# Long-convolution block: taps in 64x64 tiles, half of v turned by DMA and half loaded as rows, all table sines first

## The chip, the cores and the metric

The kernel runs on one core of a Trainium2 chip. Its time is the device time of one execution in microseconds (us). PE is TensorE (matmuls), with PEld its weight loads; DVE is VectorE, ACT is ScalarE, POOL is GpSimd, and SP issues most of the DMAs. PSUM is where matmuls write; the working memory is SBUF, with 128 partitions.

## The reference: what is computed

`q`, `k`, `v` are 2048 tokens by 512 channels, in bf16. The block normalizes `q`, shifts `k` by a four-tap filter per channel, multiplies by `v`, convolves along the tokens with a filter as long as the sequence (by FFT), multiplies by the normalized `q`, adds the input, and then runs an MLP with 1376 hidden units on the normalized result.

```python
for t in range(ks):                                   # ks = 4
    k_shift = k_shift + k_pad[:, t:t + S, :] * shift_k[:, ks - 1 - t][None, None, :]
kv = k_shift * v
...
y_f = kv_f * kf_f[None, :, :, :]                      # rfft of kv and of ssm_k, length 2 * S
...
y = y + kv * ssm_D[None, None, :]
return q * y                                          # q is layernorm(A_q)
...
h = x + _A_ref(_layernorm(x, axis=-1), A_k, A_v, A_shift_k, A_ssm_k, A_ssm_D)
h2 = h + _B_ref(_layernorm(h, axis=-1), B_w1, B_w2)   # relu(x @ w1) @ w2
```

## The kernel before

The FFT is done as matmuls with tables of sines, in two stages forward and two back. The 512 channels are four groups of 128. Tokens are numbered as 32 rows by 64. "Rows" of the data have one partition for each of 32 blocks of 64 tokens, four channel groups below each other, which makes 128 partitions.

Every engine runs its instructions in the order in which the program records them, and waits on semaphores for what the others produce. So the order of the work is written out by hand, as a list of calls at L425 to L470. PSUM work goes through `bank2` (L278), which hands out four slots of two banks each, alternating between two pools; a slot is free again when its eviction is done. DMAs run in the order of the queue that issues them.

The stages, in order of time:

- **Loads** (L99 to L130): the filter rows `kfl` in eight DMAs (four from SP, four from ACT, the last two of ACT behind the first sines), then, on SP, `k` and `v` in four chunks of 512 tokens each, both turned by the DMA so that channels lie on partitions (`kT`, `vT`), then 512 tokens of the input (`x0`) and `w1`.
- **Tables** (L133 to L269): POOL writes index patterns, DVE turns them into angles modulo one turn (`turns2`, two operations of 1024), ACT takes the sine (`sines2`) into `tab`, POOL writes the negated halves (`negated`). Two of the four tables are made ahead of stage 1, two between its blocks.
- **Stage 1 of the filter** (`stage1`, L297): eight blocks, each of 64 matmuls with 32-row weights and 64 columns, plus four small ones for the direct term. Two PSUM slots a block, one evicted by ACT and one by DVE, into `a1k`.
- **Taps** (`taps`, L335): eight groups (four chunks by two halves of the channels). A tap is a matmul with a diagonal 128x128 matrix `wdiag` (made by POOL at L209): 8 matmuls of 512 columns a group. DVE multiplies the PSUM result by `vT`, in place (L342, 1024 elements).
- **Second stage of the filter** (`second_k`, L360): 16 groups of 8 matmuls, each evicted by ACT or DVE.
- **Rows** (`to_rows`, L285): PE turns `vT` (now `kv`) from channels to tokens on partitions, eight transposes of f32 words in each of four groups, and DVE writes each to `xfl` (L290, 1024 words).
- **Paired stage 1 of the data** (`stage1_pairs`, L320), eight blocks of 32 matmuls into `a1x`, evicted by ACT and DVE. It needs all of `xfl`.
- **Products** (`product`, L484): 16 groups: two second-stage groups in PSUM, multiplied by `a1k` by DVE (L493) and by DVE or, by way of a copy `usb` of ACT (L492), by POOL (L498).
- **Inverse** (L516 to L531), **last stage and gate** (L543 to L590), and the **MLP** (L627 to L694), whose matmuls fill PE to the end.

Channel order: within each group of 128 channels, the first 64 belong to half d=0 and the other 64 to half d=1, in all four groups.

Of the kernel before, what the change touches and what calls it, by code (L numbers as in the profile page):

```python
# [9 lines left out]
ALU = mybir.AluOpType  # L10
# [5 lines left out]
P = 128  # L16
# [39 lines left out]
def kernel(  # L56
# [36 lines left out]

    kfl = front.tile([P, 64, 2, 64], BF16, name="kfl")

    def load_rows(eng, rg):
        for d in range(2):
            src = bass.AP(tensor=A_ssm_k.tensor, offset=A_ssm_k.offset + S * (P * rg + 64 * d), ap=[[64, 32], [S, 64], [1, 64]])
            eng.dma_start(out=kfl[32 * rg:32 * rg + 32, :, d, :], in_=src)  # L99

    wsh = consts.tile([P, DC, KS], BF16, name="wsh")
    nc.scalar.dma_start(out=wsh[:], in_=A_shift_k.rearrange("(r p) j -> p r j", p=P))
    scratch = rows.tile([P, 4096], I32, tag="r", name="scratch")
    drow = scratch[:, 4064:4096].bitcast(BF16)
    nc.gpsimd.memset(drow, 0.0)
# [4 lines left out]
    vT = front.tile([P, DC, S], BF16, name="vT")  # L110
    CH = 512
    kT = [front.tile([P, DC, CH + 16], BF16, name=f"kT{c}") for c in range(4)]
    nc.vector.memset(kT[0][:, :, 0:16], 0.0)
    for c in range(4):
        if c == 0:
            nc.sync.dma_start_transpose(out=kT[c][:, :, 16:CH + 16], in_=k_d[0:CH, :])
        else:
            nc.sync.dma_start_transpose(out=kT[c][:], in_=k_d[CH * c - 16:CH * c + CH, :])
        nc.sync.dma_start_transpose(out=vT[:, :, CH * c:CH * c + CH], in_=v_d[CH * c:CH * c + CH, :])

    x0 = front.tile([P, 4, D], BF16, name="x0")
    for b, src in enumerate(_tokens(x_d, 0, 4)):
        nc.sync.dma_start(out=x0[32 * b:32 * b + 32].rearrange("p t d -> p (t d)"), in_=src)


    w1 = w1p.tile([P, DC, DFF], BF16, name="w1")
    for i in range(2):
        for d in range(2):
            nc.sync.dma_start(out=w1[64 * i:64 * i + 64, 2 * d:2 * d + 2],
                                in_=B_w1.rearrange("(c i d g) f -> i d g c f", c=2, i=2, d=2)[i, d])  # L130
# [29 lines left out]
    for s in range(0, P, 64):  # L160
        nc.gpsimd.iota(n2i[s:s + 64, :], pattern=[[0, 1]], base=0, channel_multiplier=1)
    r2 = scratch[:, 0:1024].rearrange("p (a b) -> p a b", b=64)
    nc.gpsimd.iota(r2, pattern=[[2, 16], [128, 64]], base=1, channel_multiplier=0)
    ident = consts.tile([P, P], BF16, name="ident")
# [3 lines left out]

    identw = consts.tile([P, P], F32, name="identw")
    nc.gpsimd.memset(identw[:], 0.0)  # L170
    nc.gpsimd.affine_select(out=identw[:], in_=identw[:], compare_op=ALU.not_equal, fill=1.0,
                            base=0, pattern=[[-1, P]], channel_multiplier=1)

    ind = consts.tile([P, P], BF16, name="ind")
    nc.gpsimd.memset(ind[:], 0.0)
    for s in range(0, P, 32):
        nc.gpsimd.affine_select(out=ind[s:s + 32, :], in_=ind[s:s + 32, :], compare_op=ALU.not_equal, fill=1.0,
                                base=0, pattern=[[-1, P]], channel_multiplier=4)

# [11 lines left out]
    load_rows(nc.scalar, 3)  # L191
    f1hi = consts.tile([P, 64], BF16, name="f1hi")
# [10 lines left out]
    nc.gpsimd.memset(f1w[:], 0.0)  # L203
    for rg in range(DC):
        for i, f in enumerate((f1hi, f1lo)):
            nc.gpsimd.tensor_copy(out=f1w[32 * rg:32 * rg + 32, i, rg % 2, :], in_=f[32 * rg:32 * rg + 32, :])
    wdiag = rows.tile([P, DC, KS, P], BF16, name="wdiag")
    for rg in range(DC):
        nc.gpsimd.tensor_tensor(out=wdiag[:, rg, :, :], in0=ident[:].unsqueeze(1).to_broadcast([P, KS, P]),  # L209
                                in1=wsh[:, rg, :].unsqueeze(2).to_broadcast([P, KS, P]), op=ALU.mult)  # L210
    wm = rows.tile([P, 4, 344], F32, name="wm")
    ones = consts.tile([P, P], BF16, name="ones")
    nc.gpsimd.memset(ones[:], 1.0 / D)

    def turns2(i, b):
        ta = scratch[:, 1024 * (b + 1):1024 * (b + 2)].rearrange("p (a b) -> p a b", b=64)
        _turns(ta, r2, n2c[:], 8192, o2[:, i, b:b + 1])
        return ta
# [7 lines left out]

    o2 = consts.tile([P, 2, 2], F32, name="o2")
    for i in range(2):
        for b in range(2):
            nc.vector.tensor_scalar(out=o2[:, i, b:b + 1], in0=n2c[:], scalar1=32.0 * i, scalar2=4096.0 + 2048.0 * b,  # L230
                                    op0=ALU.mult, op1=ALU.add)
    for b in range(2):
        sines2(0, b, turns2(0, b))
    negated(0)
    negated(1)
# [12 lines left out]
    nc.gpsimd.iota(r3[:], pattern=[[1, 64]], base=0, channel_multiplier=0)  # L248
    for i, (top, bottom) in enumerate(((64.0, 96.0), (48.0, 80.0), (32.0, 64.0), (6144.0, 8192.0))):
        nc.gpsimd.memset(ow[0:64, i:i + 1], top)  # L250
        nc.gpsimd.memset(ow[64:128, i:i + 1], bottom)
    for i in range(3):
        nc.gpsimd.tensor_scalar(out=t3[:, i, :], in0=r3[:], scalar1=n2c[:], scalar2=ow[:, i:i + 1], op0=ALU.mult, op1=ALU.add)
    nc.gpsimd.memset(hsc[:], 0.0)
    nc.gpsimd.memset(hbi[:], 0.0)
    nc.gpsimd.tensor_scalar(out=k1o[:], in0=k1c[:], scalar1=2.0, scalar2=1.0, op0=ALU.mult, op1=ALU.add)
    for b in range(4):
        q = slice(32 * b, 32 * b + 32)
        nc.gpsimd.memset(hsc[q, b % 2:b % 2 + 1], TURN / 8192)
        nc.gpsimd.memset(hbi[q, b % 2:b % 2 + 1], -0.5 * TURN)  # L260
        nc.gpsimd.tensor_scalar(out=ofc[q], in0=k1o[q], scalar1=32.0 * (b % 2), scalar2=ow[q, 3:4], op0=ALU.mult, op1=ALU.add)
    nc.gpsimd.iota(rf[:], pattern=[[1, NT], [16, 2], [64, 32]], base=0, channel_multiplier=0)
    nc.gpsimd.tensor_scalar(out=rf[:], in0=rf[:], scalar1=k1o[:], scalar2=ofc[:], op0=ALU.mult, op1=ALU.add)
# [21 lines left out]
    def to_rows(src, q, fl):  # L285
        words = src[:].bitcast(F32).rearrange("p c (a b) -> p c a b", b=32)
        pst = bank2("pst")
        for i in range(8):
            nc.tensor.transpose(out=pst[:, i // 4, P * (i % 4):P * (i % 4) + P], in_=words[:, :, :, 8 * q + i], identity=identw[:])
        nc.vector.tensor_single_scalar(out=fl[:].bitcast(I32)[:, :, :, 8 * q:8 * q + 8],  # L290
                                       in_=pst[:].bitcast(I32).rearrange("p b (i d g) -> p g d (b i)", i=4, d=2),
                                       scalar=0, op=ALU.bitwise_or)
# [4 lines left out]
    def stage1(fl, a_out, gb, engs, spike=False):  # L297
# [9 lines left out]
        for gi in range(8):  # L307
            for f, first in ((f1hi, True), (f1lo, False)):
                for rg in range(4):
                    rw = slice(32 * rg, 32 * rg + 32)  # L310
                    nc.tensor.matmul(out=outs[rg][:, gi, :], lhsT=fl[rw, 8 * gb + gi, :, :].rearrange("p d n -> p (d n)"),  # L311
                                     rhs=f[rw, :], start=first and not spike, stop=not first,
                                     tile_position=(32 * rg, 0), skip_group_check=True)
# [6 lines left out]
    def stage1_pairs(fl, a_out, gb, engs):  # L320
        pss = [bank2("ps1") for _ in range(2)]
        for gi in range(8):
            for i in range(2):
                for h in range(2):
                    rw = slice(64 * h, 64 * h + 64)
                    nc.tensor.matmul(out=pss[h][:, gi // 4, P * (gi % 4):P * (gi % 4) + P],  # L326
                                     lhsT=fl[rw, 8 * gb + gi, :, :].rearrange("p d n -> p (d n)"),
# [7 lines left out]
    def taps(c, h):  # L335
        ps = bank2("pkv")
        for i in range(2):
            for j in range(KS):
                nc.tensor.matmul(out=ps[:, i, :], lhsT=wdiag[:, 2 * h + i, j, :],  # L339
                                 rhs=kT[c][:, 2 * h + i, 16 - j:CH + 16 - j], start=(j == 0), stop=(j == KS - 1))  # L340
        vv = vT[:, 2 * h:2 * h + 2, CH * c:CH * c + CH]
        nc.vector.tensor_tensor(out=vv, in0=ps[:], in1=vv, op=ALU.mult)  # L342
# [38 lines left out]
    s1 = lambda gb: stage1(kfl, a1k, gb, "AD", spike=True)  # L381
    tap = lambda u: taps(u // 2, u % 2)
# [11 lines left out]
    qn0 = consts.tile([P, 4, D], BF16, name="qn0")  # L394
# [3 lines left out]
    def stats(src, mv, r, q):  # L398
        for i in range(4):
            nc.vector.bn_stats(out=st[:, i, :], in_=src[:, i, :])  # L400
        for i in range(4):
# [11 lines left out]
    xfl = None  # L413

    def row(q):
        nonlocal xfl
        if xfl is None:
            xfl = rows.tile([P, 64, 2, 64], BF16, tag="r", name="xfl")
        to_rows(vT, q, xfl)
# [5 lines left out]
    s1(0)  # L425
    s1(1)
    tap(0)
    s1(2)
    sines2(1, 0, turns2(1, 0))
    tap(1)  # L430
    s1(3)
    s1(4)
    tap(2)
    s1(5)
    sines2(1, 1, turns2(1, 1))
    negated(2)
    negated(3)
    tap(3)
    s1(6)
    s1(7)  # L440
    tap(4)
# [318 lines left out]
```

## Time and profile before

| | us |
|---|---|
| runs (3) | 211.96, 212.26, 212.32; median 212.26 |
| the profiled execution, its own time | 212.53 |
| its span, first to last instruction | 210.8 |
| start of stage 1 on all filter rows | 14.6 |
| last eviction of filter stage 1 ends | 35.9 |
| last tap's multiplication starts | 47.1 |
| `xfl` complete | 56.8 |
| paired stage 1 starts | 61.5 |
| products start | 73.1 |
| first inverse block turned by DVE | 101.9 |
| MLP fills PE from | 127.5 |

The page gives the busy time of each engine, then 40 equal slices of the span (5.27 us each) with the busy share of each engine in tenths. Groups by form list, for each line, engine and shape: count, busy time, mean nanoseconds of one, then how long the engine had stood idle ahead of them and what ended it. The chain of waits follows the work that ended last back through whatever released it.

### The profile page before, as it was taken

To read this page: it belongs to the slowest core of one execution; us is meant where nothing else is said; L and a number is where in the kernel's file an instruction comes from. 1 tells how busy PE (TensorE), PEld (TensorE's weight loads), DVE (VectorE), ACT (ScalarE), POOL (GpSimd) and SP (SyncE) were. 2 spreads that over 40 slices of the span, in tenths; PEclk is the share of its full clock that TensorE was granted. 3 is DMA by queue.
4 is the path that set the end of the run, shared out by engine and by line. 5 is a ranking of instruction groups with operands and counts; after the bars stand their busy time and mean duration, and the time that the engine had idled before them with its cause. 6 is when DMAs were issued, how large, how long until landed. Compare 5 with 4: busy or idle time off the path is not lost.

```text
span 210.8 us, 4349 instructions
## 1 busy us (share of the span) xinstructions
PE 176.0 (84%) x1787; PEld 107.3 (51%) x1787; DVE 146.5 (69%) x236; ACT 93.6 (44%) x108; POOL 91.5 (43%) x109
## 2 busy tenths in 40 slices
PE   0329696998989587777796899999999999999993
PEld 0125343557768475665665564545455444444452
DVE  2615988459968689999998987988988381343042
ACT  0333535456288756651399447700560056016400
POOL 4899855402069569999298452031040002002000
PEclk9999997999999999999997999999999999999999
DMA  8999999920000000000780261251250215121012
GB/s 124 217 257 177 161 151 225 218 59 2 3 0 3 3 0 5 0 3 0 193 205 3 50 215 53 50 51 28 69 106 0 60 45 99 25 50 25 3 45 55
DMA packets 47315, 16.00 MB, mean 76 GB/s; under 512 B 42720, under 2 KB 46144, under 8 KB 47296
## 3 DMA queue, kind: packets, MB, share of 16 engines
q1 hardware_dynamic: 38400, 14.61, 35.5%
q10 hardware_dynamic: 8896, 1.12, 3.4%
q8 instruction: 14, 0.23, 0.5%
q14 instruction: 5, 0.04, 0.1%
HBM read 7.54 MB, written 2.10 MB: 46 GB/s over the span
## 4 chain that ended last, share of the span: by engine, by line
PE 59%; DVE 24%; ACT 4%; issue 4%; DMA 3%; ACTq 2%; POOL 1%; DVEq 0%; POOLq 0%
PE m L630 18%; PE m L684 17%; PE pkv L339 7%; DVE a1x L493 6%; DVE zs L523 5%; PE u L352 4%; DMA kfl<-in_A_ssm_k_dram 3%; DVE a1k L498 3%; PE pz L550 3%; PE ps L326 3%; PE ps2k L352 3%; DVE xfl L290 2%; ACT a1x L273 2%; PE pz L560 2%; DVE vT L342 2%
## 5 line engine op out<-in xcount | busy, mean ns | idle before, releaser
L666 ACT ACTIVATE h1T<-m 128x512 bf16<-128x512 f32 (+1 forms) x44 | 25.9, 597 | 43.6 <-PE m L630 43.6
L630 PE MATMUL m<-hT,w 128*128 128x512 bf16 (+1 forms) x176 | 39.0, 379 | 0.2 <-ACT hT L597 0.2
L684 PE MATMUL m<-w,h1T 128*128 128x512 bf16 (+1 forms) x165 | 36.3, 379 | 0.0
L690 DVE SCALAR_TENSOR_TENSOR o<-m,rstd,hp 128x256 bf16<-128x256 f32 x32 | 13.8, 478 | 27.6 <-PE m L684 26.6
L404 POOL TENSOR_SCALAR rstd<-mv 128x4 f32<-128x4 f32 x8 | 1.8, 228 | 71.2 <-DVE mv L402 71.2
L630 PEld LDWEIGHTS <-w 128*128 128x128 bf16 (+1 forms) x176 | 17.4, 100 | 20.4 <-issue 0.8
L498 POOL TENSOR_TENSOR a1k<-usb,a1k 128x1024 fp32r<-128x1024 f32 x10 | 23.7, 2396 | 5.3 <-DVE a1x L493 5.2
L684 PEld LDWEIGHTS <-h1T 128*128 128x128 bf16 (+1 forms) x165 | 15.9, 98 | 19.4 <-issue 0.3
L352 PE MATMUL u<-a1x,tab 64*128 64x256 f32 x256 | 19.8, 292 | 6.5 <-DVE a1x L493 2.4
L531 ACT CAST a1x<-zs 128x1024 fp32r<-128x1024 f32 (+2 forms) x10 | 17.2, 1717 | 11.9 <-DVE zs L523 11.9
L352 PEld LDWEIGHTS u<-a1x,tab 64*128 64x128 f32 x256 | 16.4, 185 | 9.8 <-issue 4.9
L493 DVE TENSOR_TENSOR a1x<-u,a1k 128x1024 fp32r<-128x1024 f32 x16 | 19.1, 1217 | 2.4 <-PE u L352 2.4
L529 POOL CAST a1x<-zs 128x1024 fp32r<-128x1024 f32 (+1 forms) x8 | 15.6, 1955 | 8.3 <-DVE zs L523 8.3
L523 DVE STREAM_TRANSPOSE zs<-pi 128x1024 f32<-128x1024 f32 x16 | 18.4, 1213 | 0.5 <-PE pi L518 0.5
L339 PE MATMUL pkv<-kT,wdiag 128*128 128x512 bf16 x64 | 18.5, 441 | 0.2 <-ACT a1k L273 0.2
L518 PE MATMUL pi<-a1k,wd 128*128 128x512 f32 x32 | 13.9, 434 | 2.9 <-DVE a1k L496 1.1
L342 DVE TENSOR_TENSOR vT<-pkv,vT 128x1024 bf16<-128x1024 f32 x8 | 9.8, 1221 | 9.2 <-PE pkv L339 8.2
L273 ACT CAST a1k<-ps2k 128x1024 fp32r<-128x1024 f32 x12 | 11.7, 1013 | 8.8 <-PE ps2k L352 8.8
L492 ACT COPY usb<-u 128x1024 f32<-128x1024 f32 x10 | 10.1, 1017 | 10.6 <-POOL a1k L498 8.7
L518 PE MATMUL pi<-a1x,wd 128*128 128x512 f32 x32 | 13.1, 408 | 0.0
L275 DVE CAST a1k<-ps 128x1024 fp32r<-128x1024 f32 x8 | 9.6, 1215 | 5.0 <-PE ps L311 5.0
L224 POOL TENSOR_SCALAR tab<-tab 128x1024 fp32r<-128x1024 f32 x4 | 11.0, 2775 | 4.4 <-ACT tab L146 4.3
(104 smaller groups left out, 268.3 us busy)
## 6 DMA issues: line engine op xcount, KB each, us to landing
xall<-in_A_q_dram SPq DMA_DIRECT2D x16, 128.0 KB, 3.3
out_dram<-o SPq DMA_DIRECT2D x62, 32.0 KB, 1.6
w<-in_B_w_dram SPq DMA_DIRECT2D x4, 344.0 KB, 7.3
w<-in_B_w_dram SPq DMA_DIRECT2D x1, 1280.0 KB, 6.2
kfl<-in_A_ssm_k_dram SPq DMA_DIRECT2D x4, 256.0 KB, 5.2
kfl<-in_A_ssm_k_dram ACTq DMA_DIRECT2D x4, 256.0 KB, 6.4
x<-in_A_q_dram SPq DMA_DIRECT2D x4, 128.0 KB, 3.8
hT<-hp SPq DMA_TRANSPOSE x7, 3.2
```

The source lines that it names most:

```text
L273: nc.scalar.copy(out=o, in_=i)
L339: nc.tensor.matmul(out=ps[:, i, :], lhsT=wdiag[:, 2 * h + i, j, :], rhs=kT[c][:, 2 * h + i, 16 - j:CH + 16 - j], start=(j == 0), stop=(j = ...
L352: nc.tensor.matmul(out=ps[:, d, 256 * i:256 * i + 256], lhsT=tab[rw, k1, b:b + 2, :].rearrange("p b k -> p (b k)"), rhs=a_in[rw, c, k1, :] ...
L493: nc.vector.tensor_tensor(out=spot(a1x, kp), in0=u2[:], in1=kk.bitcast(F32), op=ALU.mult)
L498: (nc.gpsimd if pool else nc.vector).tensor_tensor(out=kk, in0=(usb if pool else u1)[:], in1=kk.bitcast(F32), op=ALU.mult)
L518: nc.tensor.matmul(out=ps[:, b, :], lhsT=wd[:, m:m + 2, :].rearrange("p b k -> p (b k)"), rhs=src[:, d, 16 * b:16 * b + 16, c0:c0 + 32], s ...
L523: nc.vector.transpose(out=zs[:], in_=ps[:].rearrange("p b (k c) -> p c (b k)", c=32))
L529: nc.gpsimd.tensor_copy(out=o, in_=i)
L531: nc.scalar.copy(out=o, in_=i)
L630: nc.tensor.matmul(out=ps1[:fsz].rearrange("p (i t) -> p i t", i=4), lhsT=w1[:, c, fc * P:fc * P + fsz], rhs=hT[sc][:, c // 2, :, c % 2, : ...
L666: nc.scalar.activation(out=h1T[:fsz, fc, :], in_=ps1[:fsz], func=ACT.Relu)
L684: nc.tensor.matmul(out=ps2[:], lhsT=lhsT, rhs=w2[:ksz, fc, :], start=(fc == 0), stop=(fc == NFC - 1))
```

## The change

- **Channel order.** In every second group of 128 channels the two halves of 64 are exchanged (`first_channel`, `half`). The loads of the filter and of `w1`, the constant `ind` and the views of the gate and the output follow. At the output, half d=0 is now written by two operations in place of one.
- **v.** Groups 0 and 2 of `v` are turned by DMA, one DMA of 2048 tokens by 128 channels each, into `ksh`. Groups 1 and 3 are loaded as rows into `vfl`, unturned. DVE first fills all of `vfl` with ones, so that the rows of groups 0 and 2 multiply by one.
- **Taps** run as four 64x64 tiles. The two groups of a call come out with halves exchanged for one of them. DVE multiplies the even group by `ksh` in place (512 elements); ACT copies the odd group, which is only the shifted `k`, to `ksh`.
- **Rows.** 16 bf16 transposes in each of the four groups, in place of 8 of f32 words. DVE multiplies the PSUM result by `vfl` into `xfl`, in two operations of 1024. `xfl` is laid out in runs of four, so stage 1 loads its weights in steps of four elements.
- **Order.** All four tables are made ahead of stage 1; the negations, `f1w` and the turns of the inverse tables follow on POOL. Two taps stand between the blocks of stage 1 and six between the groups of the second stage. `x` is loaded behind `w1`, straight to `qn0`, and normalized in place. `scratch` is gone, its parts are tiles of their own.
- **Rest.** `usb` has three buffers instead of two. Three matmuls without use (`warm`) follow the products.

```diff
+    def load_v(r):
+        if r % 2 == 0:
+            nc.sync.dma_start_transpose(out=ksh[:, r], in_=v_d[:, P * r:P * r + P])
+        else:
+            src = bass.AP(tensor=A_v.tensor, offset=A_v.offset + P * r, ap=[[64 * D, 32], [D, 64], [1, P]])
+            nc.sync.dma_start(out=vfl[32 * r:32 * r + 32], in_=src)
...
+    ta00 = turns2(0, 0)
+    ta01 = turns2(0, 1)
     f1hi = consts.tile([P, 64], BF16, name="f1hi")
...
+    def to_rows(q, fl):
+        toks = ksh[:].rearrange("p c (a b) -> p (c a) b", b=64)
+        pst = bank2("pst")[:].rearrange("p b n -> p (b n)").bitcast(BF16)
+        for i in range(16):
+            nc.tensor.transpose(out=pst[:, P * i:P * i + P], in_=toks[:, :, 16 * q + i], identity=ident[:])
+        for d in range(2):
+            nc.vector.tensor_tensor(out=fl[:, :, d, 16 * q:16 * q + 16].rearrange("p h i l -> p i h l"),
+                                    in0=pst.rearrange("p (i d h l) -> p i d h l", d=2, h=16, l=4)[:, :, d],
+                                    in1=vfl[:, 16 * q:16 * q + 16, 64 - 64 * d:128 - 64 * d].rearrange("p i (h l) -> p i h l", l=4),
+                                    op=ALU.mult)
...
-        for i in range(2):
-            for j in range(KS):
-                nc.tensor.matmul(out=ps[:, i, :], lhsT=wdiag[:, 2 * h + i, j, :],
-                                 rhs=kT[c][:, 2 * h + i, 16 - j:CH + 16 - j], start=(j == 0), stop=(j == KS - 1))
-        vv = vT[:, 2 * h:2 * h + 2, CH * c:CH * c + CH]
-        nc.vector.tensor_tensor(out=vv, in0=ps[:], in1=vv, op=ALU.mult)
+        for j in range(KS):
+            for e in range(2):
+                for b in range(2):
+                    p = slice(64 * e, 64 * e + 64)
+                    d = e ^ b
+                    nc.tensor.matmul(out=ps[64 * d:64 * d + 64, b, :], lhsT=wdiag[p, 2 * a + b, j, :],
+                                     rhs=kT[c][p, 2 * a + b, 16 - j:CH + 16 - j], start=(j == 0), stop=(j == KS - 1),
+                                     tile_position=(64 * e, 64 * d), skip_group_check=True)
+        cs = slice(CH * c, CH * c + CH)
+        copy(eng, ksh[:, 2 * a + 1, cs], ps[:, 1, :])
+        nc.vector.tensor_tensor(out=ksh[:, 2 * a, cs], in0=ps[:, 0, :], in1=ksh[:, 2 * a, cs], op=ALU.mult)
...
+    load_k(0)
+    load_v(0)
+    load_k(1)
+    load_v(2)
+    load_k(2)
+    load_k(3)
+    nc.vector.memset(vfl[:], 1.0)
+    load_v(1)
+    load_v(3)
+    load_w1()
+    load_x0()
+    sines2(0, 0, ta00)
+    ta10 = turns2(1, 0)
+    sines2(0, 1, ta01)
+    ta11 = turns2(1, 1)
+    diagonals()
...
+    s1(0, "AD")
+    s1(1, "AD")
+    s1(2, "AD")
+    tap(0, "A")
+    s1(3, "AD")
+    s1(4, "AD")
+    tap(2, "A")
+    s1(5, "AD")
+    s1(6, "AD")
+    s1(7, "AD")
+    second_k(0, "A")
+    second_k(1, "D")
+    tap(1, "A")
...
+    pairs_pool()
+    second_k(12, "A")
     row(0)
+    second_k(13, "A")
     row(1)
+    stats(qn0, mv1, rstd1, 0)
+    second_k(14, "A")
     row(2)
+    column_means(0)
     row(3)
...
+    warm(3, w1[:, 0, 0:512])
```

## The prediction

> **What bounds the kernel now.** I read the page's slices first, then the chain of waits in order of time, then VectorE's timeline, then the groups by form.
>
> ```profile
> span 210.8 us, 4349 instructions
> ## 1 busy us (share of the span) xinstructions
> PE 176.0 (84%) x1787; PEld 107.3 (51%) x1787; DVE 146.5 (69%) x236; ACT 93.6 (44%) x108; POOL 91.5 (43%) x109
> ...
> PE   0329696998989587777796899999999999999993
> ...
> DVE  2615988459968689999998987988988381343042
> ```
>
> The 40 slices are 5.27 us each. From slice 25 on (132 us) PE is full: that is the MLP, and nothing in the change reaches it but the shape of some VectorE operations. Slices 14 to 18 are the spectral products, where DVE is full. What the change rewrites lies in the first 14 slices, where no engine is full all the time. So the question is when the products start; everything behind them moves along.
>
> ```profile
> 7.67 6.91 DMA kfl<-in_A_ssm_k_dram
> 14.63 1.03 PE ps L311 x53
> 25.61 0.51 PE ps L311 x52
> 34.65 3.49 PE pkv L339 x8
> 42.74 1.84 PE pkv L339 x8
> 51.00 2.24 DVE xfl L290 x2
> 54.54 2.27 DVE xfl L290 x2
> 61.63 0.95 PE ps L326 x32
> 73.13 1.22 PE u L352 x16
> ```
>
> The columns are start, length, what. The last rows of the filter land at 14.6 and stage 1 of the filter starts. Taps (L339) and stage 1 (L311) then alternate on PE; a tap group costs 1.84 (3.49 while the clock was low). The turned rows `xfl` are ready at 56.8, paired stage 1 of the data (L326) runs from 61.5, and the products start at 73.1. That 73.1 is the mark that I forecast.
>
> ```profile
> 10.46 0.69 DVE L152 TENSOR_SCALAR scratch<-scratch 128x1024 int32<-128x1024 int32 x1
> 15.71 2.35 DVE L275 CAST a1k<-ps 128x1024 fp32r<-128x1024 f32 x2 [4.55 <-PE ps L311]
> ```
>
> VectorE idles 4.55 us ahead of the first eviction, because the filter isn't there yet. That hole is what the change fills.
>
> **Part 1: the memset of the v rows.** In the order of the changed program VectorE does, behind the f1 casts (done at 7.93, as before: their input f1f comes at 6.9, and the two turn tables that now stand in front of them fit into the idle time up to then), a memset of `vfl`, 8192 bf16 values per partition; then both remaining turn tables; and only then the first eviction of stage 1.
>
> ```profile
> L113 DVE MEMSET kT<- 128x32 uint32 x1 | 0.1, 85 | 0.8 <-PEq L744 0.8
> L137 DVE MEMSET nbias<- 64x1 f32 x1 | 0.1, 59 | 0.0
> L342 DVE TENSOR_TENSOR vT<-pkv,vT 128x1024 bf16<-128x1024 f32 x8 | 9.8, 1221 | 9.2 <-PE pkv L339 8.2 <-DMA w<-in_B_w_dram 1.0
> L587 DVE TENSOR_TENSOR hp<-pz,qn 128x512 bf16<-128x512 f32 x2 | 1.4, 692 | 0.8 <-PE pz L550 0.7
> L588 DVE TENSOR_TENSOR hp<-hp,xall 128x1024 bf16<-128x1024 bf16 x3 | 2.1, 691 | 0.1
> ```
>
> No memset of this size is in the trace. The two small ones give (85-59)/31 = 0.84 ns per element, so 6.9 us; the multiplications from PSUM give (1221-692)/512 = 1.03 ns at one element per step, so 8.5 us; the quickest VectorE row, 1024 bf16 in 0.69 (L588, half a step each), would give some 4.3, and a form faster still about 2. I take 8.5: 26 ns are too few to fit a slope on, and both nearest rows say about one element per step. The Trainium skill, "VectorE: DVE Perf Modes", section "Zero memsets can be issued as uint32 (trn2)", has a memset at one cycle per element whatever the dtype, and a halved count for zeros alone; this one is of ones. By that rule the sum stays; without it, at 2 us, it would be 3.9 us better (a rival below).
>
> So the memset ends at 16.5, the two tables (0.80 + 0.74 each) at 19.6. VectorE's first eviction is at 19.6 instead of 15.71: 3.9 late. ScalarE's last sine (1.14) starts at 19.6, so its first eviction is at 20.8 instead of 15.66. With four PSUM slots, PE stops after two blocks of stage 1 (16.4) and waits until 21.7, and goes on with a cold clock (the 1.03 against the 0.51 above for the same block).
>
> **Part 2: stage 1.** Before, eight blocks with four taps and two tables between them are evicted from 15.7 to 35.9. After, two taps stand between them and the tables are done. VectorE: eight evictions at 1.13 (2.35 for two, above) and two half-size multiplications at 0.69 are 10.4; each of these waits for ScalarE's copy of the other half (0.59, as L666 takes for 512), some 0.9 in all; the cold PE and its slots cost some 2. That is 13.3, so the end is at 33.0, 2.9 earlier, with two taps fewer done.
>
> **Part 3: second stage and taps.** A tap was 8 matmuls of 128x128 in 1.84, 0.23 each. It becomes 16 of 64x64 in four tiles; if four run side by side it is 4 x 0.23 = 0.92. The trace shows row tiles side by side (52 matmuls of 32x128 in 0.51, under 10 ns each), but no column tiles, so the bounds are 0.85 and 16 x 0.23 = 3.7; two at a time is 1.84. I take 0.92, as the row tiles are the nearest row. Six units of two second-stage groups (8 matmuls in 0.54, from 16 in 1.15) and one tap are then 6 x 2.0 = 12.0 on PE; VectorE needs 1.13 + 0.6 a unit and ScalarE 0.93 + 0.55, so PE decides: 45.0, and 46.2 with the last copy and multiplication. Before, the last tap is multiplied at 47.1 with 8 of 16 second groups done; now it is 12.
>
> **Part 4: the rows.** Four evictions of 1024 words (1.21) become eight multiplications of 1024 bf16 with the transposes in PSUM as bf16. The two rows that bound this are L342 (1.22, PSUM) and L588 (0.69, all bf16 in SBUF); I take 1.22, the one that reads PSUM. From 46.2: tables 0.8, eight at 1.13 are 9.0, the statistics 2.4 + 0.3 stand between, waits for the second row's transposes 0.8: 59.5. The 16 transposes a row hide under it (4 x 0.24 = 0.96, from four in 0.24), as do four second groups and the column means (8.4 us of PE in 13). Paired stage 1 starts at 59.6 instead of 61.5: **1.9 earlier**, and its 11.6 to the products stay, since both copies still take one block of 1024 each.
>
> **Parts with no cost.** Queues: SP issues two transposes fewer, its four `x` loads go behind `w1`; SP was idle from 38.4 to 100.3 and the statistics need `x` at 51, so that holds unless a transposed 2048x128 slab takes over twice the 3.2 us that one of 512x512 takes in SP's queue; then taps would wait. POOL: the tables are negated by 26 and the rest of its set-up ends by 38, needed at 46. A third `usb` buffer: the loop of the products is VectorE's (4.6 busy of 4.93 per three), so nothing. The three warming matmuls (0.65) end by 98.7, but take a PSUM slot, so the first inverse halves, which ran at 98.05 and 99.30, wait for the last `a1x` product: 4 x 0.24 = 0.95 where 0.86 is free, 0.1. Sixteen more VectorE operations at the output (0.2 each) lie in 27.6 us in which VectorE waits there for PE; without that cover 3.4.
>
> **Sum.** 61.5 - 59.6 = 1.9; the 0.1 is within its error. The profiled execution took 212.53 (span 210.8 and 1.7 around it), so 210.6; it stands 0.27 above the median of 212.26, so I forecast **210.4** on the median. Its own range, from the memset at 0.84 ns (1.6 better) and from the waits that I only estimated (1.5 worse), is 208.8 to 211.9.
>
> **Rivals.**
> - *The row multiplications run at the bf16 price.* For it: all three operands are 2-byte. Against: no VectorE row here that reads PSUM is below one element per step. Eight times 0.52 is 4.2, less about 1.1 that PE then bounds: 207.4. The Trainium skill, "VectorE: DVE Perf Modes", section "The perf-mode tier table (the rule you actually need)", lists tensor_tensor with any PSUM operand at 1x, which speaks against it.
> - *The tiles take turns* (slower than before). Place: the taps. If the two column halves of a row group don't run together, a tap is 1.84 again; with 0.92 too much on eight taps, less what the early two hide, 6.5: 217, or 214 with quick rows. It decides from 1.16 us per tap on (1.9/8 above 0.92). For it: 128 weight loads in place of 64, and the trace shows no column tile. Against: row tiles overlap fully. The Trainium skill, "TensorEngine Tiling (Array Packing)", section "Restrictions and Gotchas", says that column tiling excludes the fast weight load; no run here shows that yet.
> - *The memset is short.* Stage 1 then starts on the filter at 15.7: 206.5.
> - *Strided weights.* Paired stage 1 now loads `xfl` in steps of four elements. At the f32 price (0.54/8 = 67 ns in place of 0.95/32 = 30) its blocks take 2.1: up to 216. Against: the strided f32 loads of L289 (194) cost no more than dense ones (L352, 185).
> - *PE goes cold under the row phase,* where it waits up to 3 us at a time. The trace shows 3.49 for 1.84 at a granted 0.71. Three blocks at double price, 2 us: 212.4.
>
> **Chances.** Forecast 0.42, quick rows 0.26, turns 0.14, short memset 0.08, strided 0.05, cold 0.05. The range reaches from 206.2 (quick rows and short memset) to 214.8 (turns with quick rows, part of strided); it leaves out the 217 and the far ends. Measurements of this kernel tell 0.2% from no change, 0.4 us. Faster: most of the forecast's 0.42, quick rows and short memset, 0.66. Slower: turns, strided, part of cold, a tail of the forecast, 0.26. Between: 0.08.
>
> **What would show it.** A memset of 8.5 us at 8 on VectorE and its first eviction at 19.6; a tap's 16 matmuls within 1.0; the `xfl` multiplication at 1.2; paired stage 1 from 59.6 and the products from 71.2. I am wrong if the memset is hidden by a later landing of the filter, if the taps take 1.2 or more, or if something behind the products doesn't move along.

## The result, and the profile after

The changed kernel is slower: **225.12 us** median of 4 runs (223.90 to 228.73) against 212.11 of the kernel before in the same session, a ratio of 1.0594, 95% interval 1.0534 to 1.0653. The forecast was 210.4. The profiled execution took 224.44, its span is 222.7, so the spans differ by 11.9. Ratios, here and below, leave out slow runs (over 1.5% above the fastest of their kernel; here the 228.73), so they need not be the ratio of the medians. The page, its first lines and the slices (now 5.57 us each; PEclk is the clock that PE was granted, in tenths of full speed):

```profile
span 222.7 us, 4566 instructions
PE 173.4 (78%) x1881; PEld 110.2 (49%) x1886; DVE 165.9 (74%) x261; ACT 97.0 (44%) x114; POOL 94.6 (42%) x108
...
PE   1130865998980486777789699999999999999993
...
DVE  7699574687899867999999998797997665145042
...
POOL 7779987001099201999929854222004002002000
PEclk9999996799996589999999879999999999999999
```

PE's busy time fell by 2.6 (176.0 before) and the span grew by 11.9: on PE not work but waiting was added. In the slice that begins at 66.8 (the 13th, a 0) PE stands still while POOL and DVE are both full (9). The MLP at the end is the same. The chain that ended last begins right there:

```profile
63.69 10.42 DVE qn L457 x4
74.11 1.15 DVE a1x L306
75.29 4.68 PE ps L359 x96
...
85.50 1.22 PE u L391 x16
```

Before, paired stage 1 (L326 there) ran from 61.5 and the products started at 73.13. Now PE starts paired stage 1 at 64.0, fills its four PSUM slots and waits. The products start at 85.50. What stands at the head is no matmul and no row, but the normalization of the first 512 rows of x. VectorE's timeline, with the start and the length of each group:

```profile
58.55 2.43 DVE L444 BATCH_NORM_STATS2 st<-qn 128x6 f32<-128x512 bf16 x4
60.90 0.37 DVE L449 BATCH_NORM_AGGREGATE mv<-st 128x2 f32<-128x6 f32 x4
61.17 2.51 DVE L322 TENSOR_TENSOR xfl<-pst,vfl 128x1024 bf16<-128x1024 bf16 x4
63.60 10.50 DVE L457 TENSOR_SCALAR qn<-qn,mv,rstd 128x512 bf16<-128x512 bf16 x4
74.03 2.34 DVE L306 CAST a1x<-ps 128x1024 fp32r<-128x1024 f32 x2
```

and GpSimd's in the same stretch:

```profile
62.69 11.27 POOL L417 TENSOR_TENSOR w<-w,wm 128x1376 bf16<-128x1376 bf16 x4
```

In the kernel before the same four stood at 53.16, with POOL idle:

```profile
53.16 1.38 DVE L410 TENSOR_SCALAR qn<-x,mv,rstd 128x512 bf16<-128x512 bf16 x4
```

Four operations that took some 0.4 us each now take 2072 to 2899 ns, and end with POOL's centring of w1. The change moved them: before, they stood between the second and the third row; now they stand behind the fourth, right where the centring starts. VectorE's first a1x eviction (L306, 74.03) is queued behind them, and PE behind that. From the first product on, both kernels take the same within 0.5: 74.43 to 210.8 before, 86.79 to 222.7 after.

### The profile page after: what moved, and what is told of

Read it like the earlier page. It is cut to its first block, busy times and chain, and to the rows that moved or that the text cites. A ratio compares the mean times of both kernels' runs of the same rounds, so it can differ in the third digit from the quotient of the medians.

```text
span 222.7 us, 4566 instructions
## 1 busy us (share of the span) xinstructions
PE 173.4 (78%) x1881; PEld 110.2 (49%) x1886; DVE 165.9 (74%) x261; ACT 97.0 (44%) x114; POOL 94.6 (42%) x108
## 4 chain that ended last, share of the span: by engine, by line
PE 46%; DVE 19%; ACT 2%; issue 2%; POOL 1%; DVEq 0%
PE m L722 17%; PE m L777 16%; DVE a1x L576 6%; DVE qn L457 5%; DVE zs L615 4%; PE u L391 3%; DVE a1k L581 3%; PE ps L359 3%; PE pz L642 2%; PE pi L610 2%; ACT a1x L304 2%; PE pz L652 2%; PE m L779 1%; POOL a1x L621 1%; DVE a1x L306 1%
## 5 line engine op out<-in xcount | busy, mean ns | idle before, releaser
L783 DVE SCALAR_TENSOR_TENSOR o<-m,rstd,hp 128x128 bf16<-128x128 f32 (+1 forms) x48 | 15.8, 390 | 25.6 <-PE m L777 24.8
L777 PEld LDWEIGHTS <-h1T 128*128 128x128 bf16 (+1 forms) x165 | 15.9, 98 | 19.4 <-issue 0.3
L359 PE MATMUL ps<-f1w,xfl 64*128 64x128 bf16 x256 | 9.9, 242 | 10.0 <-DVE a1x L306 9.3
L263 POOL TENSOR_SCALAR tab<-tab 128x1024 fp32r<-128x1024 f32 x4 | 16.6, 4184 | 2.5 <-ACT tab L171 2.5
L344 PE MATMUL ps<-f1hi,kfl 32*128 32x64 bf16 x256 | 8.1, 217 | 10.5 <-DMA kfl<-in_A_ssm_k_dram 6.7
L359 PEld LDWEIGHTS <-xfl 64*128 64x128 bf16 x256 | 9.3, 119 | 10.8 <-issue 10.6
L610 PE MATMUL pi<-a1x,wd 128*128 128x512 f32 x32 | 13.7, 428 | 0.0
L304 ACT CAST a1x<-ps 128x1024 fp32r<-128x1024 f32 x9 | 8.8, 1017 | 11.3 <-PE ps L359 11.3
```

Source lines behind the costliest of these rows:

```text
L263: nc.gpsimd.tensor_single_scalar(out=tab[:, 8 * i:8 * i + 8, 2:4, :], in_=tab[:, 8 * i:8 * i + 8, 0:2, :].bitcast(F32), scalar=-1.0, op=AL ...
L610: nc.tensor.matmul(out=ps[:, b, :], lhsT=wd[:, m:m + 2, :].rearrange("p b k -> p (b k)"), rhs=src[:, d, 16 * b:16 * b + 16, c0:c0 + 32], s ...
L777: nc.tensor.matmul(out=ps2[:], lhsT=lhsT, rhs=w2[:ksz, fc, :], start=(fc == 0), stop=(fc == NFC - 1))
```

## The experiments

**Theory.** VectorE's normalization and GpSimd's centring, both from SBUF to SBUF, keep each other out while they run. **Rival.** The new form is slow by itself, since it reads and writes the same tile. In each experiment the ratio is to runs of the kernel before taken beside it, whose medians lie between 212.51 and 213.35.

### Where the normalization stands, and what runs beside it

norm_late:

```diff
-    norm_rows(0, qn0, qn0)
     second_k(15, "A")
...
         stage1_pairs(...)
+    norm_rows(0, qn0, qn0)
```

> The changed kernel, with the normalization of the first 512 rows (four operations on qn0) recorded behind the eight blocks of paired stage 1 and not between the rows and them. Theory (VectorE's bf16 normalization and GpSimd's centring of w1 keep each other from SBUF when they run at the same time): the four operations are back at about 0.41 us each, VectorE evicts the first a1x block at about 64.5 and not at 74, PE's idle time of 9.3 us goes, and the products start at 75 to 77 in place of 85.5: 214 to 217. Rival (the operations are slow because they read and write the same tile): they take 10 us in the new place too, between paired stage 1 and the products, and the time stays at 224 to 226. Second rival (the hole in PE only moves, since another thing holds the products at 85): 222 to 225 with short operations.

213.29, a ratio to before of 0.9999 (0.9968 to 1.0030), a little under the 214 to 217 that were expected. The four take 1.38, although they still write in place.

norm_apart:

```diff
-    norm_rows(0, qn0, qn0)
+    norm_rows(0, kT[0][:, :, 0:512], qn0)
```

> The changed kernel, with the four normalizations in the same place but written to another tile (the first chunk of k, no longer needed by then); their result is not used, so the gate works with rows that are not normalized. Theory (VectorE and GpSimd exclude each other): nothing changes, the four still take about 10 us, 224 to 226. Rival (reading and writing the same tile is slow): they take 1.5 to 1.7 us, 214 to 217.

224.19, ratio 1.0497 (1.0430 to 1.0565); the four take 2097 to 2891 ns. Not writing in place helps nothing.

no_center:

```diff
-    for n in (0, 1):
-        center(n)
     norm_rows(0, qn0, qn0)
     second_k(15, "A")
     column_means(1)
-    for n in (2, 3):
-        center(n)
```

> The changed kernel with the centring of w1 on GpSimd (four operations of 2.85 us) left out, so w1 is used as it was loaded; the normalization stays where it is. Theory (exclusion): the four normalizations take 1.4 to 1.7 us in their old place, and the time is 214 to 217. Rival (same tile read and written): the four still take 10 us, 224 to 226. If the time goes below norm_late's by over 1 us, the centring costs something beside this as well.

213.95, ratio 1.0038 (0.9998 to 1.0078). VectorE's timeline of no_center:

```profile
60.69 2.49 DVE L322 TENSOR_TENSOR xfl<-pst,vfl 128x1024 bf16<-128x1024 bf16 x4
63.09 1.37 DVE L457 TENSOR_SCALAR qn<-qn,mv,rstd 128x512 bf16<-128x512 bf16 x4
64.58 4.76 DVE L306 CAST a1x<-ps 128x1024 fp32r<-128x1024 f32 x4
```

The same operation in the same place takes 1.37 once POOL is idle, and its first product starts at 76.16, not at 86.79: 10.6 earlier, as its span is 10.6 shorter (212.1). Of that 9.45 is the eviction that waits (64.58 against 74.03). The other 1.2 lies between this eviction and the first product (12.76 in place of 11.58), where PE's granted clock is 0.50 to 0.59 after the 9.3 us in which it stood still.

before_beside:

```diff
-    norm_rows(0, qn0, x0)
     row(2)
...
         center(n)
+    norm_rows(0, qn0, x0)
     seconds(range(14, 16), "AD")
```

> The kernel before, with only its four normalizations (from x0 to qn0, not in place) moved from between the second and third row to behind the record of the centring. Theory (exclusion): four operations of 2 to 2.9 us instead of 0.41, from about 60 on, ahead of VectorE's first a1x eviction; 219 to 223, slower than before by 7 to 10. Rival (in place is what is slow): 211.5 to 213.5, no change.

223.10, ratio 1.0466 (1.0399 to 1.0532), just above the expected 219 to 223. This one move alone gives the old kernel most of the loss of the whole change. VectorE's timeline of before_beside:

```profile
59.46 11.04 DVE L410 TENSOR_SCALAR qn<-x,mv,rstd 128x512 bf16<-128x512 bf16 x4
70.43 1.21 DVE L275 CAST a1k<-ps2k 128x1024 fp32r<-128x1024 f32 x1
```

and GpSimd's:

```profile
59.11 11.24 POOL L378 TENSOR_TENSOR w<-w,wm 128x1376 bf16<-128x1376 bf16 x4 [1.74 <-ACT wm L374]
```

So the theory holds in four ways, and the rival falls with norm_late and norm_apart. POOL loses nothing (2.85 each, 2.83 before); each of VectorE's four lasts as long as one of POOL's. The Trainium skill, "SBUF — State Buffer", section "Who interferes with whom", states the rule: the two engines share one pair of SBUF ports, which whoever issues first holds for the whole instruction. The runs agree: 406 ns alone, 2886 beside an instruction of 2850. Not every VectorE operation suffers: in late_ones, below, four evictions that read PSUM (L306, 61.45 to 66.21) lie beside the same centring (59.03 to 70.30) and take 4.76, as in no_center without it.

With that loss gone the kernel is where it was before (0.9999), and not 0.9% faster, as was forecast. The rest of the study is about this remainder.

### The fill of ones

late_ones is norm_late with the fill on GpSimd, in the stretches of partitions that need it:

```diff
-    nc.vector.memset(vfl[:], 1.0)
...
     inverse_turns()
+    for p in (0, 64):
+        nc.gpsimd.memset(vfl[p:p + 32], 1.0)
```

> norm_late (normalization behind paired stage 1), and the ones for groups 0 and 2 of v are written by GpSimd into the two stretches of 32 partitions that need them, behind its table work, and no longer by VectorE's memset of the whole tile. Theory (the memset of 6.9 us and the tables it delays hold the first evictions of stage 1 until 21, and GpSimd's first negation with them): the first evictions are at 15.7 to 17, stage 1 ends 3 to 5 us earlier, and all of it reaches the products, which start at 70 to 73: a ratio to the kernel before of 0.977 to 0.988, 208 to 210.5. Rival (the hole of 2 us in PE's own stream and the filter chunks that come late decide, not the evictions): under 1 us, ratio 0.995 to 1.0. GpSimd's two fills should take 6 to 8 us each and end by 52, ahead of the first row.

211.06, ratio 0.9960 (0.9910 to 1.0009): short of the theory's ratio, and in the rival's range. The traces put it between the two. The first eviction came as expected, at 15.89 in place of 21.07, yet stage 1 was only evicted by 33.7: it takes 17.8 from its first eviction in place of 15.9, so 2 of the 5.2 us are lost inside it. The other 3 reach the products, as the theory said: the first starts at 73.03, where no_center, with the fill still on VectorE, has 76.16, and the span is 209.1 against 212.1. Against the kernel before (74.43, span 210.8) only 1.4 to 1.7 of that is a gain, since no_center starts its products 1.7 later than that kernel. GpSimd's fills took 13.9 for both (33.4 to 47.3), and its four negations 11.7 where the changed kernel has 16.6.

ones_pool is the same edit in the changed kernel, with the normalization left beside the centring:

> The changed kernel with only the fill of ones moved from VectorE to GpSimd as in late_ones; the normalization stays beside the centring. If the two losses add up: 3 to 5 us under the changed kernel, 220 to 222, ratio 1.037 to 1.046, with the four normalizations still at 10 us. If the earlier rows give the normalization a place before the centring, it would be far less, 209 to 212.

221.51, ratio 1.0413 (1.0352 to 1.0473), with the four at 10.52: the two losses add up. By the spans the fill costs 3.0 here too (222.7 and 219.7).

### What takes part of it back

In late_ones PE's timeline has a stop in the middle of a block of stage 1 that waits for nothing the trace shows ("issue"; the number ahead of it is the idle time):

```profile
26.55 0.24 PE L344 MATMUL ps<-f1hi,kfl 32*128 32x64 bf16 x4 [3.75 <-issue]
```

A shorter one, of 0.99, ends at 21.46. The changed kernel has one as well, of 1.94, that ends at 34.07. Counted in program order (68 matmuls a block of stage 1, 16 a tap), the stops of all these kernels fall ahead of matmul 220, 348, 476 and 604: 128 apart, 256 instructions with the weight loads. The page of the changed kernel has a queue of its own for instructions:

```profile
q8 instruction: 15, 0.25, 0.5%
```

Its columns are packets, MB and share. 0.25 MB in 15 packets are some 16 KB each, and PE's 1886 weight loads with as many matmuls are 14.7 times 256. Every such stop ends 2.3 to 3.0 us behind a packet of that queue: in late_ones the packets stand at 19.00 and 24.28 and the stops end at 21.46 and 26.55, in the changed kernel it is 31.12 and 34.07. So PE stops where a block of its own instructions ends and the next is late. The packets come some 4 to 6 us apart while data is loaded. The Trainium skill, "Runtime: NRT & Kernel Launch", section "Instruction fetch mechanics", has the blocks (16 KiB, 256 instructions) and calls the cost of crossing one "mostly hidden". The block agrees; here it is not hidden.

late_ones_w1 holds back the last loads, to see whether the loads make the instructions late:

```diff
-    load_w1()
-    load_x0()
...
     s1(7, "AD")
+    nc.vector.memset(w1[:, :, 0:1], 0.0)
+    load_w1()
+    load_x0()
```

> late_ones, with the loads of w1 and of the first 512 rows of x held back until stage 1 of the filter has been evicted (by a small memset into w1 that they have to follow), so that less is loaded while stage 1 runs. Theory (PE's hole of 2 us in the middle of a stage 1 block is a load of its own instructions that waits behind the data): the hole goes or falls under 1 us, and the time is 1 to 2 us under late_ones unless another hole opens under the later loads. Rival (the hole has nothing to do with the loads): hole and time as in late_ones, within 0.5 us; slower by 1 to 3 us if the column means or the statistics then wait for w1 and x.

212.31, ratio 0.9934 (0.9893 to 0.9975), a stop of 3.44: no change. But that stop ended at 27.4, and in late_ones those loads are issued from 29.7 on, so holding them back could not reach it. quiet7 and quiet5 hold all that follows the second chunk of k, quiet7 behind s1(7) as shown, quiet5 behind s1(5):

```diff
     load_k(1)
-    load_v(2)
-    load_k(2)
-    load_k(3)
-    load_v(1)
-    load_v(3)
-    load_w1()
-    load_x0()
...
     s1(7, "AD")
+    nc.vector.memset(ksh[:, 2, 0:2], 0.0)
+    load_v(2)
...
+    load_x0()
```

> late_ones, with every load behind the second chunk of k (two of k, the second half of v, both of the rows of v, w1 and x) held until stage 1 of the filter is evicted (by a memset of two columns that they have to follow), so that nothing is loaded from about 22 until then. Theory (PE waits for blocks of its own instructions, 128 matmuls with their weight loads each, that come late because the loads fill the DMA engines): the holes at about the 220th, 350th and 500th matmul after 12 us, 4.7 us in late_ones, go; stage 1 is evicted by 28 to 30 in place of 33.7. The taps then wait for their loads, so the total is no test: 207 to 214. Rival (PE's holes have another cause, such as a limit of its own in reading instructions): the holes stay at the same matmuls, with 3 to 4 us, and stage 1 ends at 33 to 34.

213.65, ratio 1.0059 (1.0024 to 1.0094). The theory was half right. With the DMA engines at 0.03 of their time between 22 and 30, the stops are still there, 1.04 and 2.38, and stage 1 is evicted by 32.1, not 28 to 30. The packets come 3.5 to 3.7 us apart there instead of 4 to 6: the loads make it worse, but a block takes that long without them.

> As quiet7, but the loads are held only until the sixth of the eight blocks of stage 1 has been evicted by VectorE. Theory (instructions late behind loads): the holes up to there go, stage 1 is evicted by 28 to 30, the second half of v lands some 6 us behind, by 31 to 33, and the taps keep up: 2 to 4 us under late_ones, ratio to before 0.978 to 0.988. Rival (another cause): holes as in late_ones, the loads come later on top, ratio 0.996 to 1.02.

210.86, ratio 0.9896 (0.9849 to 0.9944), between the theory and the rival: the stops as in quiet7, and two new waits of VectorE, 1.86 for the second half of v and 1.77 for x.

no_lo asks whether the count of instructions is what limits stage 1:

```diff
-            for f, first in ((f1hi, True), (f1lo, False)):
+            for f, first in ((f1hi, True),):
...
```

> late_ones, with stage 1 of the filter using only the upper part of its table (f1hi): the matmuls with the lower part f1lo are left out, so the filter is rounded more coarsely. It halves the instructions of a block (36 matmuls in place of 68) and takes 0.25 us of PE from a block that its evictions (1.0 and 1.2 us) hide anyway. Theory (PE gets its instructions in blocks of 128 matmuls some 4 to 5 us apart and runs out of them): the holes at the 349th and 500th matmul fall beyond stage 1, which is evicted by 27 to 29.5 in place of 33.7, and the time is 3 to 6 us under late_ones, ratio to before 0.967 to 0.983. Rival (another limit holds stage 1, such as the evictions or the loads): it ends at 32 to 34, ratio 0.99 to 1.0.

**206.99**, ratio 0.9713 (0.9676 to 0.9750), 4.1 under late_ones. Stage 1 is evicted by 27.8 and PE has no stop of this kind. That is the theory's case. It is no version to keep, since it rounds the filter.

mix4 moves two taps from the second stage back into stage 1:

```diff
     s1(3, "AD")
-    s1(4, "AD")
     tap(2, "A")
+    s1(4, "AD")
+    tap(1, "A")
     s1(5, "AD")
+    tap(3, "A")
     s1(6, "AD")
...
     second_k(1, "D")
-    tap(1, "A")
...
     second_k(3, "D")
-    tap(3, "A")
```

> late_ones, with four taps between the blocks of stage 1 as the kernel before has, in place of two; the two are taken from the second stage, where PE is full. Theory (instructions in blocks): 32 more matmuls ahead of the end of stage 1 cost a quarter of a block, some 1.2 us there, and the 2 x 1.06 us of taps go from the full phase, so 0.5 to 1.5 us are won, ratio to before 0.988 to 0.993. Rival (the stops are of fixed length, whatever work is ahead): stage 1 ends 2 us later, which the two taps give back: no change, 0.994 to 0.998. If the second half of v isn't there in time for the added taps: slower than late_ones by 1 to 3 us.

212.70, ratio 0.9984 (0.9945 to 1.0022), a miss for both. The timeline of its PE shows why:

```profile
36.32 0.24 PE L344 MATMUL ps<-f1lo,kfl 32*128 32x64 bf16 x4 [2.10 <-issue]
```

Eight blocks and four taps are 608 matmuls, so matmul 604 lies four ahead of the end of stage 1: the whole last block waited 2.1 us for four matmuls, on top of the stop of 3.43 at 26.67. Stage 1 ended at 37.9, 4.1 later than in late_ones. What costs is not only how many instructions there are, but where a block of them ends.

quiet4x holds the loads one block less than quiet5, and puts x ahead of the rows of v:

```diff
     s1(4, "AD")
+    nc.vector.memset(ksh[:, 2, 0:2], 0.0)
+    load_v(2)
+    load_k(2)
+    load_k(3)
+    load_x0()
+    load_v(1)
+    load_v(3)
+    load_w1()
```

> quiet5, with the loads held one block less (until the fifth block is evicted by VectorE), and the first 512 rows of x loaded ahead of the rows of v and of w1. Theory: the holes stay at the 1.0 and 2.4 us of quiet5, stage 1 is evicted by 32 to 33, VectorE's waits for the second half of v (1.86) and for x (1.77) go, and the products start 2.5 to 3.5 us earlier than in quiet5: 207.5 to 209, ratio to before 0.974 to 0.983. Rival (the earlier loads bring the longer holes back): as late_ones, 0.99 to 0.997.

**208.87**, ratio 0.9805 (0.9738 to 0.9873): faster than both kernels, and it computes what they do. The stops are 0.87 and 2.11, stage 1 is evicted by 30.6, the waits of quiet5 are gone, and the first product starts at 70.95 (73.34 in quiet5, 74.43 before).

### The turning of the rows

late_ones_dense is late_ones with

```diff
-            nc.tensor.transpose(..., in_=toks[:, :, 16 * q + i], ...)
+            nc.tensor.transpose(..., in_=toks[:, P * (16 * q + i):P * (16 * q + i) + P], ...)
```

on the flat view of ksh.

> late_ones, with the 64 transposes reading 128 neighbouring columns of ksh each instead of columns 64 apart; it leaves out the right order of the tokens, so it convolves other numbers, and its time alone counts. Theory (weights read in steps of 64 elements make the 16 transposes of a row take 1.6 us and PE the bound of the row phase): 16 take 0.95 to 1.05, the row phase is 1.5 to 2.5 us shorter, ratio to before 0.008 to 0.012 under that of late_ones. Rival (the transposes are set by their moving columns, or VectorE is the bound there): no difference, under 0.5 us.

209.21, ratio 0.9804 (0.9748 to 0.9860). PE's weight loads by form, in the changed kernel:

```profile
L320 PEld LDWEIGHTS <-ksh 128*128 128x128 bf16 x64 | 6.2, 204 | 1.3 <-DVE ksh L381 1.0
```

and in late_ones_dense:

```profile
L320 PEld LDWEIGHTS <-ksh 128*128 128x128 bf16 x64 | 3.7, 98 | 0.9 <-issue 0.5
```

Loading weights 64 elements apart takes 204 ns in place of 98, and 16 transposes take 1.65 in place of 1.06. By the traces the first product starts 1.2 earlier (71.87 against 73.03), and from the last tap's multiplication to the last row it takes 9.1 in place of 10.4, so the 1.5 to 2.5 that were expected are not quite reached. The medians are 1.9 apart and the ratios 3.3 us, each ratio within half a per cent.

## Why the prediction was wrong

- **The step that failed** is the move of the normalization. In part 4 only the statistics "stand between" the rows; "Parts with no cost" has SP's and POOL's queues, but not that `norm_rows` passes from ahead of the third row to a place beside the centring. Not even its 1.4 is in the sum. Beside the centring it cost 10.6, by the spans of no_center and the changed kernel. No rival had it.
- **Part 1, the memset:** forecast 8.5, measured 6.88, the slope of the two small ones (0.84 ns an element), which the forecast named and set aside. VectorE idled 1.66 ahead of it, with nothing in the trace that it waited for, and the two tables behind it took 4.1 in place of 3.1, beside POOL's negations. First eviction 21.07, forecast 19.6. POOL's first negation, which starts inside the memset, takes 8.0 instead of 2.8, and 3.5 in late_ones, which has no such memset. There the tables lie elsewhere too, so that the memset itself keeps POOL out is not shown.

```profile
L485 DVE MEMSET vfl<- 128x8192 bf16 x1 | 6.9, 6885 | 1.7 <-issue 1.7
L263 POOL TENSOR_SCALAR tab<-tab 128x1024 fp32r<-128x1024 f32 x4 | 16.6, 4184 | 2.5 <-ACT tab L171 2.5
```

- **Part 2, stage 1:** forecast end 33.0, measured 36.95. The forecast let evictions, and PE by its matmul times, set the pace. From late_ones on it is the supply of PE's instructions. Of the 4.0 by which the changed kernel ends late, 1.5 lie ahead of the first eviction, and the stop is 1.94. Behind that stop its granted clock is 0.50 from 35 to 41. (The kernel before has 0.50 to 0.54 from 34.65 to 38.1 too, without such a stop, so that the stop lowers the clock is not shown.) The kernel before has the same 576 matmuls up to here and no such stop over 0.5. Its taps fill 1.84 us with 8 matmuls, so, as I read it, it asks for instructions hardly faster than they come. The gain that part 2 counted was in part not to be had.
- **Part 3, taps:** the cost was right. Four tiles run side by side, 1.06 for 16 matmuls (forecast 0.92, deciding point of the rival 1.16); a unit takes 2.13 (forecast 2.0). The first unit ran at the granted clock of 0.50: 2.08 for its two second groups, 1.92 for its tap. The last tap is multiplied by 53.3, forecast 46.2; of these 7.1, stage 1 is 4.0 and the first unit 1.9.
- **Part 4, rows:** the rival of quick rows came true. The group of VectorE:

```profile
L322 DVE TENSOR_TENSOR xfl<-pst,vfl 128x1024 bf16<-128x1024 bf16 x8 | 5.3, 713 | 1.9 <-POOL wd L300 1.1 <-PE pst L320 0.8
```

It reads PSUM and takes 0.71 for 1024, as the bf16 row in SBUF does (0.69). The Trainium skill, "VectorE: DVE Perf Modes", section "The perf-mode tier table (the rule you actually need)", lists tensor_tensor with any PSUM operand at 1x; here, with bf16 in PSUM, the measurement differs from that row, and the measurement decides. The transposes, costed at 0.96 a row and hidden, take 1.65 and bound the phase instead, with PE. It took 10.4 in place of 13.3.
- **The other rivals:** taps in turn, the short memset and dear strided weights for paired stage 1 are refuted (its matmuls take 242 ns in the changed kernel, in part on the low clock, and 217 in late_ones, against 216 before). PE's granted clock did fall, to 0.50, but behind stage 1 and behind the normalization; in the rows it is 1.00.
- **Two readings of the clock** in the forecast don't hold. The tap of 3.49 stands at a granted 0.53 over its own 3.49 us, not 0.71. The first block's 1.03 (0.51 later) stands at a granted 1.00, so the granted clock does not explain that price, and what does stays open. The "some 2" for a cold PE in part 2 rests on that second reading.
- **Behind the products** nothing was lost or won over 0.5 us, as forecast.

The sum: 10.6 for the normalization, and 1.3 for the rest (212.1 for no_center against 210.8 before) where -1.9 was forecast. Those 3.2 are what is left of the 6.6 by which no_center's last tap is late on the forecast (52.8 against 46.2), after the rows gave back 2.9 (complete at 63.2 against 59.5) and the part behind them 0.5.

## What to carry to other kernels

When an order of calls is rewritten, list every operation whose neighbours in time have changed, above all each VectorE operation from SBUF to SBUF that comes to lie beside a GpSimd one (here it was `tensor_scalar`, on bf16 and on int32), and cost it at the length of the GpSimd operation. A stretch of many short matmuls has a floor that no engine's busy time shows: divide its matmuls by 128 and allow 3.5 us for each, and 4 to 6 while data is loaded; a faster engine or an earlier start only lets PE reach that floor. When a speed-up moves the time less than it should, look for "issue" on PE at equal distances in the count of its instructions.

## What the runs showed that was not expected

- A very short operation can be held as well: in no_lo VectorE's operation on 192 int32 values, 0.25 elsewhere, fell beside GpSimd's fill of ones and ended with it. VectorE's timeline, then GpSimd's:

```profile
43.63 3.54 DVE L297 TENSOR_SCALAR t<-t 128x192 int32<-128x192 int32 x1
```

```profile
33.16 13.89 POOL L503 MEMSET vfl<- 32x8192 bf16 x2
```

- GpSimd's fill of 8192 values takes 6.9 us on 32 partitions, as VectorE's does on 128: 0.85 and 0.84 ns an element of a partition.
- Blocks of 128 matmuls' instructions come 3.5 to 3.7 us apart on idle DMA engines, some 4 to 6 under load. In quiet7 the next packet moves 1.1 to 1.2 after PE has started on a block, and PE starts on the following one 2.4 to 2.6 behind that packet. Why it takes so long even then stays open.
